# A planned queue order, in-place global keys and values, and matmuls of zeros at the start of an attention and feed-forward kernel

## The chip, the core and the metric

The kernel runs on one core of one Trainium2 chip. A core has engines that each execute their own instructions strictly in the order in which the program issues them, and that wait for one another by semaphores: TensorE (PE in the profile; PEld is its weight load), VectorE (DVE), ScalarE (ACT), GpSimd (POOL), and SyncE (SP), which here issues all DMA transfers. Transfers move data between the chip's memory and the on-chip SBUF; matmuls write to PSUM, which has eight banks of 2 KB per partition. The metric is the time of one execution on the device in microseconds (us); lower is better.

## The reference

Four batches, eight heads, 768 positions, head dimension 64. Each position attends to the last 96 positions (itself included) and to the first eight positions of its sequence, the global ones, with a bias that grows with the distance. The result is a matrix of 3072 tokens by 512, which goes through a feed-forward layer that takes the maximum of three products.

```python
rel = pos[:, None] - pos[None, :]
is_global = pos[None, :] < 8
is_local = (rel >= 0) & (rel < 96)
keep = is_global | is_local
dist = np.where(is_global & ~is_local, 96.0, np.abs(rel))
scores = q @ k.T / 8 - slopes[:, None, None] * dist      # per head
a = softmax(np.where(keep, scores, -1e9))
x = (a @ v).transpose(0, 2, 1, 3).reshape(3072, 512)
h = np.maximum(np.maximum(x @ w1, x @ w2), x @ w3)       # 512 -> 768
out = h @ w_out                                          # 768 -> 512
```

## The kernel before

The 3072 tokens are 24 tiles of 128, six per batch. A tile T attends to its own 128 keys and to the 128 keys before it (tile T-1, in which the first eight keys are replaced by the global ones, so that 128 columns hold both). A tile passes through these units, which the text names by a letter and the tile, with a half g of four heads after the point where there are two:

- **load** (L, line 108): three transfers of q, k and v, 256 KB each, into one of six buffers `raw`.
- **cast** (C, lines 110 to 117): POOL turns q and k into bf16 in one instruction (`qkb`) and v in a second (`va`).
- **X** (lines 139 to 151): eight PE transposes of q and k into PSUM, one ACT copy to `qkT`. Then POOL makes the key and value tiles that the *next* tile will see: `kgT`, a copy of the keys with the eight global columns laid over it (lines 136 and 137), and `vg`, the same for the values (lines 125 and 126).
- **S** (lines 153 to 183): eight small matmuls for four heads, an exponential on ACT into `P`. The multiplication of `P` by the mask `wmask` on DVE (line 182) is issued one unit later.
- **A** (lines 185 to 209): the product of `P` with the values of both tiles, then a reciprocal and a multiplication on DVE into `xb`.
- **T** (lines 211 to 220; the function is `u_XT`): four transposes and a DVE copy into `xT`.

The feed-forward layer works on chunks of tiles, of sizes 4, 2, 2, 4, 4, 4, 4. **F c.f.j** (line 231) is the product of chunk c with 128 columns of weight j: four matmuls that are 512 wide (256 in the chunks of two tiles). For j = 0 ACT copies the result, for j = 1 and 2 DVE takes the maximum with it (lines 238 and 240). **F2** (lines 243 to 252; O in the order of the change) is the second product of one tile: six 512-wide matmuls into the PSUM bank `po`, an ACT copy to `ost`, and a store.

The weights arrive in fp32 as three groups w0, w1 and w2 (three transfers of 512 KB each, one per j) and `w_out` (three of 512 KB). Their casts (W) are on ACT, DVE and POOL for j = 0, 1 and 2, those of `w_out` (Q) on ACT.

The order on the engines is the order in which the program issues its units, and so is the order of the loads in SP's queue. Line 318 lists the loads: tiles 0 to 3, w0, w1, tile 4, w2, tile 5, w_out, and then tiles 6 and on. X(T) is followed by the casts of tile T+1, and by the loads up to tile T+5 (lines 380 to 383). The attention units of all tiles form one list (lines 337 to 359), in which X of the next tile stands before the last units of the tile at hand: X4 stands before the second half of A3 and before T3. The attention units of chunk 0 go first; from then on they are spread evenly between the feed-forward units of the chunk before (lines 402 to 426). The second products of a chunk stand between the feed-forward groups of the next one; those of the last chunk come at the end, one after another.

The PSUM banks: `sp` two banks (scores), `h0`, `h1`, `h2` (feed-forward, and in the first four tiles also scores and transposes), `op`, `tp` (transposes of X and T), `po`.

Of the kernel before, what the change touches and what calls it, by code (L numbers as in the profile page):

```python
# [15 lines left out]
ALU = mybir.AluOpType  # L16


@with_exitstack
def kernel(  # L20
# [42 lines left out]
    kg_pool = ctx.enter_context(tc.tile_pool(name="kg", bufs=3))  # L63
# [23 lines left out]
    vg_ring = [persist.tile([128, H * 65], BF16, name=f"vg{i}") for i in range(3)]  # L87
# [4 lines left out]
    raw, qb, kb, qkT, kgT, Pt, ops, xb, rzs = {}, {}, {}, {}, {}, {}, {}, {}, {}  # L92
    xT = {}
    va, vg = {}, {}
# [14 lines left out]

    def cast(T):  # L110
        b, t = divmod(T, NT)
        r = raw[T]
        qk = cast_pool.tile([128, 2, DM], BF16, name="qkb", tag="qkb")
        qb[T] = qk
        nc.gpsimd.tensor_copy(qk, r[:, 0:2].rearrange("p a h d -> p a (h d)"))  # L115
        va[T] = va_first[b % 2] if t == 0 else va_ring[T % NVA]
        nc.gpsimd.tensor_copy(heads(va[T])[:, :, 0:D], r[:, 2])  # L117

    def make_vg(T):
        b, t = divmod(T, NT)  # L120
        if t == 0:
            vg[T] = va[T]
        elif t < NT - 1:
            vg[T] = vg_ring[T % 3]
            nc.gpsimd.tensor_copy(words(vg[T]), words(va[T]))
            nc.gpsimd.tensor_copy(words(vg[T][0:NG]), words(va[b * NT][0:NG]))

    def make_kg(T):
        b, t = divmod(T, NT)
        kT = qkT[T][:, 1]  # L130
        if t == 0:
            kgT[T] = kT
            nc.gpsimd.tensor_copy(kg8[b % 2], kT[:, :, 0:NG])
        elif t < NT - 1:
            kgT[T] = kg_pool.tile([128, NP, 128], BF16, name="kgT", tag="kgT")
            nc.gpsimd.tensor_copy(words(kgT[T]), words(kT))  # L136
            nc.gpsimd.tensor_copy(kgT[T][:, :, 0:NG], kg8[b % 2])

    def u_X(T):
        if T < NSTART and T % 2:  # L140
            tp = psH.tile([128, 2, NP, 128], BF16, name="tph", tag="h2")
        else:
            tp = psT.tile([128, 2, NP, 128], BF16, name="tp", tag="tp")
        for a in range(2):
            for jp in range(NP):
                nc.tensor.transpose(tp[:, a, jp], qb[T][:, a, jp * 128:(jp + 1) * 128], identb)  # L146
        qkT[T] = qkT_pool.tile([128, 2, NP, 128], BF16, name="qkT", tag="qkT")
        nc.scalar.copy(qkT[T], tp)  # L148
        make_kg(T)
        make_vg(T)  # L150
        return []

    def u_S(T, g):
        b, t = divmod(T, NT)
        alt = T < NSTART and g == 1
# [6 lines left out]
        for ds in range(2 if t else 1):  # L162
            for j2 in range(2):
                jp = 2 * g + j2
                for hh in range(2):
                    hsl = slice(64 * hh, 64 * hh + 64)
                    st = qkT[T][hsl, 1, jp] if ds == 0 else kgT[T - 1][hsl, jp]
# [13 lines left out]
        if t:  # L181
            return [lambda: nc.vector.tensor_mul(P, P, wmask[:, g])]  # L182
        return [lambda: nc.vector.tensor_mul(P[:, :, 0], P[:, :, 0], wmask0[:, g])]

    def u_A(T, g):
        b, t = divmod(T, NT)
        if T < NSTART and g == 1:
            op = psP.tile([128, 4, 65], FP32, name="opp", tag="po")
        else:
            op = psO.tile([128, 4, 65], FP32, name="op", tag="op")  # L190
        P = Pt[T, g]
        for j2 in range(2):
            for hh in range(2):
# [5 lines left out]
                if t:  # L199
                    nc.tensor.matmul(o, P[:, i, 1], heads(vg[T - 1])[:, h], start=False, stop=True,  # L200
                                     skip_group_check=True)
# [7 lines left out]
        return []  # L209

    def u_XT(T):
# [3 lines left out]
        tp = psT.tile([128, NP, 128], BF16, name="xtp", tag="tp")  # L215
# [4 lines left out]
        return []  # L220
# [4 lines left out]
    def u_F1(c, f, j):  # L225
# [15 lines left out]
        return []  # L241

    def u_F2(c, tt):
        po = psP.tile([128, DM], FP32, name="po", tag="po")
        for f in range(NF):
            nc.tensor.matmul(po, ht[c][:, f, tt * 128:(tt + 1) * 128], wo[:, f],  # L246
                             start=(f == 0), stop=(f == NF - 1))
        ost = ost_pool.tile([128, DM], FP32, name="ost", tag="ost")
        nc.scalar.copy(ost, po)  # L249
        T = chunks[c][tt]  # L250
        nc.sync.dma_start(out=out[T * 128:(T + 1) * 128, :], in_=ost)
        return []
# [5 lines left out]
    def load_w(g):  # L258
        for j in range(3):
            st = stage_pool.tile([128, 4, 256], FP32, name="wst", tag="wst")  # L260
            wst[g, j] = st
            nc.sync.dma_start(out=st, in_=wsrc[j][:, g * 256:(g + 1) * 256].rearrange(  # L262
                "(i p) f -> p i f", p=128))

    def load_wo():
        for i in range(3):
            st = stage_pool.tile([128, 2, DM], FP32, name="wst", tag="wst")
            wst["o", i] = st
            nc.sync.dma_start(out=st, in_=moe_w_out[i * 256:(i + 1) * 256, :].rearrange(
                "(i p) f -> p i f", p=128))  # L270

    def cast_w(g):
        nc.scalar.copy(w123[g][:, :, 0], wst[g, 0])
        nc.vector.tensor_copy(w123[g][:, :, 1], wst[g, 1])
        nc.gpsimd.tensor_copy(w123[g][:, :, 2], wst[g, 2])
# [3 lines left out]

    with tc.manual_schedule():  # L280
        load(0)

# [25 lines left out]
        for h in range(H):  # L308
# [8 lines left out]

        loads = [("T", T) for T in range(1, NSTART)] + [("w", 0), ("w", 1), ("T", NSTART),
                                                        ("w", 2), ("T", NSTART + 1), ("o",)]
        loads += [("T", T) for T in range(NSTART + 2, NTT)]  # L320
        done = [0]

        def upto(*what):
            if what[0] == "T" and what[1] >= NTT:
                return
            while what in loads[done[0]:]:
                x = loads[done[0]]
                done[0] += 1
                if x[0] == "T":
                    load(x[1])  # L330
                elif x[0] == "w":
                    load_w(x[1])
                else:
                    load_wo()


        att = []
        for i in range(NSTART):
            att.append(("X", i))
            if i >= 1:  # L340
                att += [("A", i - 1, 0), ("A", i - 1, 1)]
            att += [("S", i, 0), ("S", i, 1)]
            if i >= 1:
                att.append(("T", i - 1))
        i = NSTART - 1
        att += [("A", i, 0), ("X", i + 1), ("A", i, 1), ("S", i + 1, 0), ("T", i)]
        for i in range(NSTART, NTT + 1):
            if i < NTT and i > NSTART:
                att.append(("S", i, 0))
            if i > NSTART:  # L350
                att.append(("A", i - 1, 1))
            if i < NTT:
                att.append(("S", i, 1))
            if i + 1 < NTT:
                att.append(("X", i + 1))
            if i < NTT:
                att.append(("A", i, 0))
            if i > NSTART:
                att.append(("T", i - 1))

        deferred = []

        def tick():
            ready = [d for d in deferred if d[0] <= 0]
            rest = [(n - 1, fn) for n, fn in deferred if n > 0]
            deferred.clear()
            deferred.extend(rest)
            for _, fn in ready:
                fn()

        def emit_att(u):
            tick()
            if u[0] == "S":
                for fn in u_S(u[1], u[2]):
                    deferred.append((0, fn))
            elif u[0] == "A":
                u_A(u[1], u[2])
            elif u[0] == "X":
                T = u[1]
                u_X(T)  # L380
                if T + 1 < NTT:
                    cast(T + 1)
                upto("T", T + 5)
            else:
                u_XT(u[1])

        pos = 0

        def att_until(stop):
            nonlocal pos  # L390
            while pos < len(att):
                u = att[pos]
                emit_att(u)
                pos += 1
                if u == stop:
                    break

        upto("T", 3)
        cast(0)
        att_until(("T", chunks[0][-1]))  # L400
        cast_w(0)
        for c in range(NCH):
            ffn = []
            for f in range(NF):
                ffn += [(u_F1, (c, f, j)) for j in range(3)]
                if c and f >= 1 and f <= len(chunks[c - 1]):
                    ffn.append((u_F2, (c - 1, f - 1)))
            if c + 1 < NCH:
                end = att.index(("T", chunks[c + 1][-1])) + 1
            else:  # L410
                end = len(att)
                ffn += [(u_F2, (c, tt)) for tt in range(len(chunks[c]))]
            n = end - pos
            slots = len(ffn) - 2
            start = pos
# [47 lines left out]
```

## Time and profile before

| | us |
|---|---|
| median of three runs | 216.99 (216.52 to 217.34) |
| the profiled execution | 216.65 |
| its span, from first to last instruction | 214.9 |
| TensorE busy | 182.7 (85%) |
| VectorE busy | 121.5 (57%) |
| ScalarE busy | 113.0 (53%) |
| GpSimd busy | 66.1 (31%) |

The profile's times are those of one execution, counted from the first instruction. "Busy" counts the time in which an engine has an instruction at work; matmuls overlap, so that a full TensorE is not necessarily at its peak. In a row of the timeline the columns are the start, the duration, the engine, the source line, the operation, `out<-in`, the shapes and the count of merged instructions; in brackets stands how long the engine had idled before it, and what released it. In a row of groups the last columns are the busy time, the mean duration of one in ns, and the idle time in front of the group. In the chain of waits a row has only the start, the duration and what the time went to.

### The profile page before, as it was taken

What the parts mean: (1) busy time and instruction counts of PE and PEld (TensorE: products, weight loads), DVE (VectorE), ACT (ScalarE), POOL (GpSimd) and SP (SyncE); (2) the same over time, 40 slices, a digit from 0 to 9 for tenths busy, and PEclk for the clock granted to TensorE, in tenths of its full rate; (3) what the DMA queues carried; (4) which work ended last, traced back from release to release, by engine and by line L of the source; (5) the groups of instructions that cost most, each with busy time, mean ns of one, the idle gap of its engine ahead of it and who ended that gap; (6) DMA issues with size and microseconds to landing.
All of it is one profiled execution on the core that took longest, in us unless ns stands there. A gap on an engine that the chain in (4) does not pass through costs nothing.

```text
span 214.9 us, 4230 instructions
## 1 busy us (share of the span) xinstructions
PE 182.7 (85%) x1640; PEld 103.1 (48%) x1640; DVE 121.5 (57%) x266; ACT 113.0 (53%) x165; POOL 66.1 (31%) x131
## 2 busy tenths in 40 slices
PE   0446825998999999789999999999999999999962
PEld 0335622543566776466555455545544555444420
DVE  2164714576674648875876878565765666532400
ACT  5855504775765756566657635565564552233231
POOL 4654322437405047135433703135505000000000
PEclk9999999999999999999999999999999999999999
DMA  7999999999999894889547980111101111012122
GB/s 151 219 218 338 319 247 274 344 193 221 219 208 222 221 259 80 195 187 196 112 110 172 232 175 0 52 49 50 52 0 52 49 49 52 2 49 83 64 100 98
DMA packets 83924, 31.73 MB, mean 148 GB/s; under 512 B 75456, under 2 KB 80064, under 8 KB 83904
## 3 DMA queue, kind: packets, MB, share of 16 engines
q1 hardware_dynamic: 83904, 31.46, 64.1%
q8 instruction: 13, 0.21, 0.4%
q14 instruction: 7, 0.06, 0.1%
HBM read 25.17 MB, written 6.29 MB: 146 GB/s over the span
## 4 chain that ended last, share of the span: by engine, by line
PE 60%; SPq 17%; ACT 10%; DMA 4%; DVE 4%; issue 2%; POOL 1%; ACTq 0%
PE h L231 35%; PE po L246 14%; SPq L108 13%; ACT P L178 5%; DMA raw<-in_v_dram 4%; PE sp L168 4%; SPq L262 3%; DVE P L182 3%; PE xtp L218 2%; ACT qkT L148 2%; PE tp L146 2%; PE op L197 2%; ACT h L236 1%; ACT ost L249 1%; PE op L200 1%
## 5 line engine op out<-in xcount | busy, mean ns | idle before, releaser
L231 PE MATMUL h<-xT,w 128*128 128x512 bf16 (+1 forms) x504 | 110.7, 353 | 3.1 <-DVE xT L219 1.6
L231 PEld LDWEIGHTS <-w 128*128 128x128 bf16 x504 | 44.0, 98 | 35.9 <-issue 1.8
L178 ACT ACTIVATE P<-sp 128x1024 bf16<-128x1024 f32 (+1 forms) x44 | 42.1, 958 | 21.6 <-PE sp L168 21.6
L182 DVE TENSOR_TENSOR P<-P,wmask 128x1024 bf16<-128x1024 bf16 x40 | 33.6, 845 | 25.0 <-ACT P L178 24.6
L238 DVE TENSOR_TENSOR h<-h,h 128x512 bf16<-128x512 bf16 (+1 forms) x42 | 25.5, 608 | 29.0 <-PE h L231 28.4
L246 PE MATMUL po<-wo,ht 128*128 128x512 bf16 x144 | 35.0, 379 | 2.2 <-ACT ost L249 2.2
L236 ACT CAST h<-h 128x512 bf16<-128x512 f32 (+1 forms) x42 | 22.2, 528 | 22.5 <-PE h L231 22.2
L249 ACT COPY ost<-po 128x512 f32<-128x512 f32 x24 | 14.1, 586 | 37.2 <-PE po L246 34.1
L115 POOL CAST qkb<-raw 128x1024 bf16<-128x1024 f32 x24 | 24.8, 1034 | 15.7 <-DMA raw<-in_k_dram 15.7
L148 ACT COPY qkT<-tp 128x1024 bf16<-128x1024 bf16 x22 | 22.3, 1014 | 13.2 <-PE tp L146 13.2
L240 DVE TENSOR_TENSOR ht<-h,h 128x512 bf16<-128x512 bf16 (+1 forms) x42 | 25.5, 608 | 5.2 <-PE h L231 3.3
L146 PE MATMUL tp<-identb,qkb 128*128 128x128 bf16 x176 | 14.9, 234 | 13.6 <-POOL qkb L115 10.7
L136 POOL COPY kgT<-qkT 128x256 int32<-128x256 int32 x16 | 6.7, 416 | 59.7 <-ACT qkT L148 59.7
L146 PEld LDWEIGHTS <-qkb 128*128 128x128 bf16 x192 | 13.8, 108 | 19.8 <-POOL qkb L115 14.7
L246 PEld LDWEIGHTS <-ht 128*128 128x128 bf16 x144 | 13.2, 98 | 16.0 <-issue 3.0
L207 DVE TENSOR_TENSOR xb<-op,rz 128x256 bf16<-128x256 f32 x44 | 18.7, 424 | 1.5
L197 PEld LDWEIGHTS <-P 128*128 128x128 bf16 x192 | 15.0, 103 | 7.7 <-DVE xb L207 2.3
L168 PE MATMUL sp<-qkT 64*128 64x128 bf16 x204 | 14.1, 231 | 3.7 <-ACT qkT L148 2.9
L168 PEld LDWEIGHTS <-qkT 64*128 64x128 bf16 x224 | 7.6, 101 | 19.5 <-issue 15.7
L197 PE MATMUL op<-va,P 128*128 128x65 bf16 x148 | 14.6, 198 | 2.5 <-DVE xb L207 1.5
L200 PEld LDWEIGHTS <-P 128*128 128x128 bf16 x160 | 12.2, 103 | 2.4
L117 POOL CAST va<-raw 128x512 bf16<-128x512 f32 x20 | 12.7, 635 | 0.1
(52 smaller groups left out, 128.8 us busy)
## 6 DMA issues: line engine op xcount, KB each, us to landing
raw<-in_q_dram SPq DMA_DIRECT2D x24, 256.0 KB, 5.0
raw<-in_k_dram SPq DMA_DIRECT2D x24, 256.0 KB, 5.0
raw<-in_v_dram SPq DMA_DIRECT2D x24, 256.0 KB, 5.0
out_dram<-ost SPq DMA_DIRECT2D x24, 256.0 KB, 2.0
wst<-in_moe_w_dram SPq DMA_DIRECT2D x9, 512.0 KB, 6.5
wst<-in_moe_w_out_dram SPq DMA_DIRECT2D x3, 512.0 KB, 5.4
```

The source lines that it names most:

```text
L108: nc.sync.dma_start(out=r[:, i], in_=src[b, :, sl, :].rearrange("h s d -> s h d"))
L115: nc.gpsimd.tensor_copy(qk, r[:, 0:2].rearrange("p a h d -> p a (h d)"))
L146: nc.tensor.transpose(tp[:, a, jp], qb[T][:, a, jp * 128:(jp + 1) * 128], identb)
L148: nc.scalar.copy(qkT[T], tp)
L168: nc.tensor.matmul(sps[hh][:, j2, ds], st, qkT[T][hsl, 0, jp], start=True, stop=True, skip_group_check=True)
L178: nc.scalar.activation(P[:, :, 0:n], sp.rearrange("p a b d n -> p (a b) d n")[:, :, 0:n], AF.Exp, bias=0.0, scale=scale)
L182: return [lambda: nc.vector.tensor_mul(P, P, wmask[:, g])]
L197: nc.tensor.matmul(o, P[:, i, 0], heads(va[T])[:, h], start=True, stop=(t == 0), skip_group_check=True)
L231: nc.tensor.matmul(ps, w123[f // 2][:, dm, j, (f % 2) * 128:(f % 2) * 128 + 128], xT[c][:, dm], start=(dm == 0), stop=(dm == 3))
L238: nc.vector.tensor_max(h01s[c, f], h01s[c, f], ps)
L240: nc.vector.tensor_max(ht[c][:, f], h01s[c, f], ps)
L246: nc.tensor.matmul(po, ht[c][:, f, tt * 128:(tt + 1) * 128], wo[:, f], start=(f == 0), stop=(f == NF - 1))
```

## The change

The lists and counters that made the order are gone. A text, `SCHEDULE`, names 470 units, and a loop issues them in that order:

```python
units = {"L": load, "w": load_w, "o": load_wo, "C": cast, "X": u_X, "S": u_S, "M": u_M,
         "A": u_A, "G": put_kg, "V": put_vg, "T": u_XT, "F": u_F1, "W": cast_w,
         "Q": cast_wo, "O": u_F2, "E": u_E}
for u in SCHEDULE.split():
    units[u[0]](*(int(n) for n in u[1:].split(".") if n))
```

The units are finer than before: the casts of a tile are two (C T.0 for q and k, C T.1 for v), the mask multiplication is one of its own (M), so are the loads and casts of each weight (w, W) and the two copies of global keys (G) and values (V). Its beginning, and further parts of it:

```
C0.0 X0 L1 S0.0 C1.0 M0.0 S0.1 G0 X1 C0.1 S1.0 S1.1 M0.1 L2 C2.0 X2 M1.0 C1.1 G1 M1.1 A0.0 L3 C3.0
C2.1 A0.1 S2.0 S2.1 X3 L4 L5 M2.0 A1.0 A1.1 T0 w0.0 w0.1 G2 S3.0 M2.1 w0.2 w1.1 C4.0 V1 M3.0 X4 S3.1
A2.0 A2.1 M3.1 T1 G3 S4.0 w1.0 C3.1 w1.2 W0.0 L6 V2 w2.0 w2.1 C5.0 A3.0 A3.1 T2 M4.0 w2.2 L7 X5 S4.1
T3 F0.0.0 W0.1 F0.0.1 W0.2 F0.0.2 W1.1 F0.1.0 o0 C4.1 V3 F0.1.1 G4 F0.1.2 A4.0 W1.0 W1.2 S5.0 M4.1
M5.0 F0.2.0 C6.0 F0.2.1 A4.1 C5.1 F0.2.2 S5.1 M5.1 F0.3.0 V4 T4 F0.3.1 W2.0 F0.3.2 W2.1 o1 X6 F0.4.0
W2.2 A5.0 S6.0 F0.4.1 A5.1 S6.1 F0.4.2 F0.5.0 C7.0 T5 M6.0 F0.5.1 M6.1 X7 C6.1 C7.1 F0.5.2 A6.0 Q0
G6 F1.0.0 S7.0 F1.0.1 F1.0.2 F1.1.0 A6.1 F1.1.1 o2 Q2 M7.0 F1.1.2 F1.2.0 T6 S7.1 G7 L8 F1.2.1 A7.0
C8.0 Q1 L9 F1.2.2 F1.3.0 F1.3.1 M7.1 C9.0 X8 L10 O0.0 S8.0 L11 A7.1 C8.1 F1.3.2 M8.0 L12 L13 F1.4.0
F1.4.1 X9 S8.1 G8 M8.1 F1.4.2 O0.1 F1.5.0 S9.0 V7 F1.5.1 T7 A8.0 C10.0 L14 C9.1 M9.0 O0.2 X10 A8.1
...
F5.5.1 F5.5.2 T23 O4.3 F6.0.0 F6.0.1 F6.0.2 F6.1.0 F6.1.1 F6.1.2 F6.2.0 F6.2.1 O5.0 F6.2.2 O5.1
F6.3.0 F6.3.1 F6.3.2 O5.2 F6.4.0 O5.3 F6.4.1 F6.4.2 F6.5.0 F6.5.1 F6.5.2 E
```

The other parts, as diffs. The global keys and values are written into the tile's own buffers instead of copies, after its own attention has read them:

```diff
-            kgT[T] = kg_pool.tile([128, NP, 128], BF16, name="kgT", tag="kgT")
-            nc.gpsimd.tensor_copy(words(kgT[T]), words(kT))
-            nc.gpsimd.tensor_copy(kgT[T][:, :, 0:NG], kg8[b % 2])
+            nc.gpsimd.tensor_copy(kT[:, :, 0:NG], kg8[b % 2])
...
+    def put_vg(T):
+        b, t = divmod(T, NT)
+        if 0 < t < NT - 1:
+            nc.gpsimd.tensor_copy(words(va[T][0:NG]), words(va[b * NT][0:NG]))
```

For the first four tiles the cast of q moves to DVE, X always uses the bank `tp`, and T uses the bank `h2`:

```diff
-        nc.gpsimd.tensor_copy(qk, r[:, 0:2].rearrange("p a h d -> p a (h d)"))
...
+        if T < 4:
+            nc.vector.tensor_copy(qk[:, 0], flat[:, 0])
+            nc.gpsimd.tensor_copy(qk[:, 1], flat[:, 1])
+        else:
+            nc.gpsimd.tensor_copy(qk, flat[:, 0:2])
...
-        if T < NSTART and T % 2:
-            tp = psH.tile([128, 2, NP, 128], BF16, name="tph", tag="h2")
-        else:
-            tp = psT.tile([128, 2, NP, 128], BF16, name="tp", tag="tp")
+        tp = psT.tile([128, 2, NP, 128], BF16, name="tp", tag="tp")
...
+        where_xt = 'h2' if early(T) else 'tp'
```

The last chunk's second products go to four different banks, two tiles at a time, the sixth matmul of a tile after the first five of both; the copies of the last two tiles are split between ACT and DVE:

```diff
+    spare = ["po", "op", "tp", "sp"]
...
+            tag = spare[tt % 4] if c == last else "po"
...
+        if T >= NTT - 2:
+            for i, copy in enumerate((nc.scalar.copy, nc.vector.tensor_copy)):
+                sl = slice(i * 256, (i + 1) * 256)
+                copy(ost[:, sl], po[:, sl])
...
+    def u_E():
+        n = len(chunks[last])
+        for tt in range(0, n, 2):
+            two = range(tt, min(tt + 2, n))
+            for x in two:
+                f2_mm(last, x, range(NF - 1))
+            for x in two:
+                f2_mm(last, x, [NF - 1])
+                f2_out(last, x)
```

And right behind the first load, ahead of everything else, PE multiplies zeros:

```diff
         load(0)
+            zeros = persist.tile([128, 512], BF16, name="zeros")
+            nc.vector.memset(zeros, 0.0)
+            wp = psO.tile([128, 512], FP32, name="wp", tag="op")
+            for _ in range(13):
+                nc.tensor.matmul(wp, zeros[:, 0:128], zeros, start=True, stop=True)
```

The other strings of casts in POOL's order that the text below names stand in parts of `SCHEDULE` that are left out here.

More of the change, by code (lines that the diff above doesn't have):

```diff
@@ L19 @@
+"""
 @with_exitstack
@@ L240, in u_F1 @@
             nc.vector.tensor_max(ht[c][:, f], h01s[c, f], ps)
-        return []
-    def u_F2(c, tt):
[L244 to L252, printed above, removed]
+    pos_ = {}
@@ L254 @@
+    def u_F2(c, tt):
+        f2_mm(c, tt, range(NF))
+        f2_out(c, tt)
     wsrc = [moe_w1, moe_w2, moe_w3]
     wst = {}
[L258 to L270, printed above, removed]
@@ L315 @@
                                  scale=-slopes[h])
[L318 to L334, printed above, removed]
@@ L337 @@
[L337 to L359, printed above, removed]
@@ L361 @@
[L361 to L385, printed above, removed]
```

142 lines of the change are left out of this document (69 added, 73 removed).

## The prediction

> **What bounds the kernel now.** I read the slices of the page first (forty of 5.4 us), then the busy time by stage, then the chain of waits and the timeline where a stage is thin.
>
> ```profile
> PE   0446825998999999789999999999999999999962
> ```
>
> TensorE (PE) is nearly full from slice 9 on, and thin before. The same in five stages (columns: window, its length, then busy us of PE, PEld, DVE, ACT, POOL, the granted clock, DMA share, GB/s):
>
> ```profile
> 0.00:35.60 35.60, 15.16 (x176) 11.77 (x176) 14.85 (x40) 19.49 (x36) 15.83 (x39) 1.00 1.13 254
> 35.60:49.30 13.70, 12.23 (x97) 5.84 (x97) 8.09 (x17) 8.54 (x10) 5.34 (x7) 1.00 1.14 259
> 49.30:60.00 10.70, 10.70 (x78) 5.38 (x79) 6.91 (x15) 6.61 (x9) 6.12 (x10) 1.00 1.09 220
> 60.00:203.20 143.20, 138.88 (x1270) 77.99 (x1268) 90.98 (x194) 76.06 (x106) 38.78 (x76) 1.00 0.48 110
> 203.20:214.90 11.70, 5.70 (x25) 2.13 (x22) 0.69 (x1) 2.35 (x4) 0.00 (x0) 0.97 0.25 91
> ```
>
> The first 60 us have PE holes while the DMA share is full; from 60 to 203.2 us PE idles 143.20 - 138.88 = 4.3 us: no order of the same matmuls can take more than that out of this stage. The front and the tail are what can move. The front, from the timeline and, for the last three rows, the chain of waits:
>
> ```profile
> 29.68 1.04 POOL L115 CAST qkb<-raw 128x1024 bf16<-128x1024 f32 x1 [4.62 <-DMA raw<-in_k_dram]
> ...
> 30.78 1.03 PE L146 MATMUL tp<-identb,qkb 128*128 128x128 bf16 x8 [4.00 <-POOL qkb L115]
> ...
> 35.28 0.42 DVE L219 COPY xT<-xtp 128x512 bf16<-128x512 bf16 x1
> ...
> 35.75 1.86 PE L231 MATMUL h<-xT,w 128*128 128x512 bf16 x4 [1.64 <-DVE xT L219]
> ...
> 40.42 1.03 PE L231 MATMUL h<-xT,w 128*128 128x512 bf16 x4
> ...
> 60.05 0.69 DVE L240 TENSOR_TENSOR ht<-h,h 128x512 bf16<-128x512 bf16 x1
> ```
>
> ```profile
> 38.79 8.79 DMA raw<-in_v_dram
> ...
> 47.64 0.62 POOL vaf L117
> ...
> 48.26 0.99 POOL w L275
> ```
>
> Tile 4's loads stand in SP's queue behind two weight groups, so its cast starts at 29.68. Its transposes stand in PE's order ahead of tile 3's last attention and ahead of T3, whose copy is the row at 35.28, and the first feed-forward group (F0.0.0) starts only at 35.75. Then the weight cast at 48.26, which F0.2.2 needs, stands in POOL's order behind a cast of tile 6 that waits for its load: PE stops until 49.30. Chunk 0's feed-forward ends with the maximum at 60.05.
>
> ```profile
> 6.51 1.03 PE L146 MATMUL tp<-identb,qkb 128*128 128x128 bf16 x8 [6.51 <-POOL qkb L115]
> ...
> 7.75 0.99 ACT L148 COPY qkT<-tp 128x1024 bf16<-128x1024 bf16 x1
> ```
>
> Those two rows are tile 0's start: its transposes and their copy.
>
> **The front after the change.** Bytes decide it: a tile is 3 x 256 KB = 0.786 MB, a weight group (three transfers) 1.57 MB. The DMA rates by window, same columns:
>
> ```profile
> 2.00:16.00 14.00, 4.69 (x52) 3.65 (x53) 5.03 (x13) 9.23 (x25) 7.30 (x15) 1.00 1.32 222
> 16.00:26.00 10.00, 7.23 (x88) 5.66 (x87) 6.28 (x14) 5.67 (x8) 4.25 (x10) 1.00 1.11 336
> 26.00:30.00 4.00, 0.62 (x8) 0.46 (x8) 1.64 (x5) 0.35 (x1) 0.32 (x1) 1.00 1.04 175
> ```
>
> Tiles 0 to 3 (3.1 MB) land by 16 us at 222 GB/s; the weights that follow move at 336; tile 4's remainder crawls at 175, and from 49.3 on tiles run at 220 (stage row). The new SP order is tiles 0 to 5, w0, w1, tile 6, w2, tile 7, w_out, tile 8. Six tiles: 2 + 4.72/0.222 = 23.3 us. w0 lands at 23.3 + 1.57/0.336 = 28.0, w1 at 32.7, tile 6 at 36.2 (222 GB/s) to 37.2 (175), w2 at 40.9 to 41.9, tile 7 at 45.4. The unit lengths (groups of instructions, then the chain of waits):
>
> ```profile
> L178 ACT ACTIVATE P<-sp 128x1024 bf16<-128x1024 f32 x37 | 38.0, 1026 | 17.3 <-PE sp L168 17.2
> L148 ACT COPY qkT<-tp 128x1024 bf16<-128x1024 bf16 x22 | 22.3, 1014 | 13.2 <-PE tp L146 13.2
> L273 ACT CAST w<-wst 128x1024 bf16<-128x1024 f32 x3 | 3.1, 1044 | 0.0
> L275 POOL CAST w<-wst 128x1024 bf16<-128x1024 f32 x3 | 3.1, 1039 | 0.0
> L274 DVE CAST w<-wst 128x1024 bf16<-128x1024 f32 x3 | 2.1, 685 | 0.0
> ```
>
> ```profile
> 50.55 0.86 PE h L231 x4
> ...
> 68.91 0.33 PE sp L168 x8
> ...
> 73.06 0.45 PE tp L146 x8
> ...
> 88.75 0.44 PE h L231 x4
> ...
> 199.35 1.29 PE po L246 x6
> ```
>
> Attention of tiles 0 to 3 is off the end's path as long as it keeps step with the loads. ACT is its fullest engine: a tile takes a copy of 1.01 and two exponentials of 1.03, 3.1 us, against 0.786/0.222 = 3.5 us for its load. It takes up tile 0 at 7.75, after the mask's exponentials, and would be through S4.0 at about 23 (the short tile 0 some 2.5, tiles 1 to 3 with their waits 3.5 each, then the copy of X4 and one exponential), 1 us and more ahead of w0.0 (23.3 + 1.6 = 24.9). F0.0.0 then waits for ACT's weight cast, 24.9 + 1.04 = 25.9; F0.0.2 for POOL's, 28.0 + 1.04 = 29.1, and ends at 30.0. From there 15 groups of 0.86 (12.9 us) and, in PE's order, A4, A5, S5, S6, T4, T5, X6, X7 remain before F0.5.2 ends: two X at 0.45, two S at 0.33, two shorter S and four A and two T at about 0.25 each (estimates, scaled from the 0.33 and 0.45), 3.5 us. Together 16.4 us, 46.4. (Check: the old kernel did 10 groups and 8 such units in its full stage 49.30 to 60.00, 8.6 + 1.9 = 10.5 of 10.7 us.) The last cast of w2 bounds it from the other side: 41.9 + 1.04 = 42.9, and F0.4.2 to F0.5.2 with T5 and X7 is 4.1 us behind, 47.0. I take 47.0, and 47.5 with the clock below: **12.4 us** earlier than 59.95, with the same work done but one short A. Bounds: 45.5 (weights at the 360 or so that 336 averages down) to 53 (loads at 175 after every weight group, and the cold groups).
>
> **The zeros.** Thirteen 512-wide matmuls at 1.86/4 = 0.46 us cold take 6.0 us, beginning about 1 us in, when PE has nothing to do (first transposes at 6.5). Worst cost: 0.6 us of delay to X0, hidden, since ACT's copy of X0 cannot start before 7.75. What they bring: the groups at 35.75 (1.86) and 40.42 (1.03) are the same instruction, slow before and quick after some 4 us of dense PE work, while the granted-clock column says 1.00 in both windows. If PE is slow at 25.9, F0.0.0 to F0.0.2 run back to back at 1.86 and end near 31 instead of 30.0: 1 us. If it is quick, nothing. I take 0.5. The Trainium skill, "TensorE: Matmul & The Clock Gate", Part 1, says the array runs at half rate until about 3.4 us of sustained work and falls back after an idle window of that length. By that rule the zeros' warmth is gone by the first 3.4 us gap among the loads, and the sum would be 0.5 us worse than mine; the trace agrees with the rule's first half (4 us), and shows gaps of 4.00 us at 30.78 with slow matmuls behind.
>
> **In-place keys and values.** Gone are the copies to kgT and vg, per tile 0.40 + 0.41 us on POOL, 16 of each:
>
> ```profile
> L136 POOL COPY kgT<-qkT 128x256 int32<-128x256 int32 x16 | 6.7, 416 | 59.7 <-ACT qkT L148 59.7
> L125 POOL COPY vg<-va 128x260 int32<-128x260 int32 x16 | 6.5, 406 | 0.0
> ```
>
> 13.2 us of POOL, off the path (POOL is busy 38.78 of 143.20): worth 0 by itself. The small copies stay and now wait: G(T), which overwrites eight keys, for S(T.1), and S(T+1) waits for G(T); V(T) for A(T.1), and A(T+1) for V(T). Behind them in POOL's queue stand casts of later tiles. From tile 6 on the PE work standing between S(T.1) and S(T+1.0) in the written order is at least 1.5 us, between A(T.1) and A(T+1.0) at least 1.2, against at most 0.41 for the copy: 0, unless a 1.03 or 0.61 cast stands just ahead, then up to 0.5 a tile.
>
> **The middle.** Loads first: tile 7 lands at 45.4, w_out at 50.1, the keys of tile 8 at 52.5, and the cast ends at 53.6. PE comes to X8 11 groups of 0.44 and 1.4 us of attention after F0.5.2, at 53.8: level. X9 is about 3.6 us behind both ways. So 0 to 3 us of waiting, I take 1; from tile 11 on the loads run ahead, also where an output transfer stands before a load in SP's queue (O0.0 before L11). The written order leaves S, A, X and T of a tile apart by more than their ACT and DVE steps almost everywhere, so of the 4.3 us idle I take 3 back. Against it, DVE:
>
> ```profile
> 84.19 2.87 DVE L182 TENSOR_TENSOR P<-P,wmask 128x1024 bf16<-128x1024 bf16 x1
> ...
> 87.53 0.68 DVE L182 TENSOR_TENSOR P<-P,wmask 128x1024 bf16<-128x1024 bf16 x1
> ```
>
> ```profile
> 84.93 1.03 POOL L115 CAST qkb<-raw 128x1024 bf16<-128x1024 f32 x1
> 85.91 0.61 POOL L117 CAST vaf<-raw 128x512 bf16<-128x512 f32 x1
> ```
>
> The mask multiply takes 2.87 instead of 0.68 while POOL runs casts one after another, and ends 0.5 us after the last of them (85.91 + 0.61): 2.2 us lost. The new POOL order has such rows (C13.0 C14.0 C12.1 C13.1; C15.1 C16.1 C17.1 C17.0; C19.0 C18.1 C20.0 C21.0), 3 to 4 us each. PE can work on for some 1 to 2 us; I take 1 us in all. The middle: 3 - 1 - 1 = **1 us**, bounds -4 and +4.3.
>
> **The tail.**
>
> ```profile
> 203.07 1.46 PE L246 MATMUL po<-wo,ht 128*128 128x512 bf16 x6
> ...
> 204.61 0.59 ACT L249 COPY ost<-po 128x512 f32<-128x512 f32 x1 [2.48 <-PE po L246]
> 205.25 1.46 PE L246 MATMUL po<-wo,ht 128*128 128x512 bf16 x6 [0.72 <-ACT ost L249]
> ...
> 211.13 0.59 ACT L249 COPY ost<-po 128x512 f32<-128x512 f32 x1 [1.59 <-PE po L246]
> ```
>
> Four output groups share one PSUM bank, so each waits for the copy before it: 203.24 to 211.72, 8.5 us. With four banks: 4 x 1.29 = 5.2, plus 0.2 for the last matmul to drain (1.46 - 1.29), plus a copy halved over ACT and DVE, 0.3 to 0.6, with semaphores 5.9. The wait for the last maximum (0.69) is covered by ten matmuls of two groups. The last two stores now come together: 0.2 back. **2.4 us**, bounds 1.8 to 2.8.
>
> **Sum.** The profiled execution took 216.65 us, 1.75 beside its span of 214.9; the median of the runs is 0.34 above it. 12.4 + 1 + 2.4 = 15.8: 200.9 on that scale, 201.2 on the median's; I forecast **201.0 us**, own range 198 to 205.
>
> **Rivals.** (a) Late loads: tiles at 175 GB/s after weights, not 222, cost 1 us each for tiles 6 to 8, and the waits at X8 to X10 grow by 3: 205 to 209. For it 26 to 30 us; against it 220 GB/s from 49.3 on. Chance 0.12. (b) The mask multiply behind strings of casts: 2.2 us lost on DVE, less 1 us of cover, 1.2 on PE each. Three to five such cases give 4 to 6 us, 204.6 to 207; chance 0.13. The Trainium skill, "SBUF — State Buffer", says in its sections on contention that a VectorE instruction with two SBUF inputs and a GpSimd instruction that reads SBUF exclude one another; the rows at 84 us agree (2.87 against 0.68). (c) The same mechanism on the other side: slower than before needs over 15 us, 13 of the 30 multiplies from tile 7 on, each held by a cast. With 13.2 us of copies gone, POOL has fewer to hold them with. Chance 0.04, about 218 to 222. Within 0.5% of before (a bit more than a measurement here can tell from none): 0.03. (d) The middle gives back all 4.3 us and the front reaches 45.5: 14.4 + 4.3 + 2.6 = 21.3, 195.7; say 195 to 198; chance 0.13. My forecast keeps 0.55. Range: 196 to 208, which leaves out the slow tenth and part of (d). Faster: 0.55 + 0.12 + 0.13 + 0.13 = 0.93.
>
> **What would show it.** F0.0.0 near 26, F0.0.2 waiting for its POOL cast near 29, the last 512-wide maximum of chunk 0 at 47 to 48 instead of 60.05; PE busy over 97% from there to the last feed-forward group at about 189; mask multiplies of over 2 us beside POOL casts in few places; 5.9 us from there to the end of the last copy. The forecast is wrong if tile 5 lands after 25 us, if PE waits over 3 us in total at X8 to X10, or if A waits for P behind casts in more than five places.

## The result and the profile after

The changed kernel takes 203.0 us (median of four, 200.93 to 205.54) against 217.0 us: a ratio of 0.9325, 95% interval 0.9246 to 0.9403. Six later executions gave 203.36 us (202.13 to 205.7). The forecast was 201.0 us with a range of 196 to 208. The ratio, here and below, leaves out executions that lie over 1.5% above the fastest of the same kernel, and one of them is the profiled execution: 205.54 us, the longest of its four, with a span of 203.8. Where its stages differ from those of a second profile of the same kernel (span 201.4), that is said.

The busy time by stage, with the same borders as before: start of the first feed-forward group, last maximum of chunk 0, last maximum of the last chunk.

```profile
0.00:30.55 30.55, 19.93 (x205) 13.46 (x206) 15.12 (x46) 20.89 (x38) 11.66 (x28) 0.68 1.12 225
30.55:52.53 21.98, 21.89 (x157) 10.80 (x157) 15.19 (x30) 10.72 (x15) 9.23 (x13) 0.89 1.09 282
52.53:194.10 141.57, 139.67 (x1272) 79.64 (x1269) 93.53 (x196) 79.88 (x110) 32.87 (x58) 0.99 0.57 124
194.10:203.80 9.70, 5.14 (x24) 2.16 (x22) 1.44 (x3) 1.72 (x4) 0.00 (x0) 0.93 0.28 108
```

The reader is to see three gains. Chunk 0 ends at 52.53 instead of 60.05: 7.5 us. The middle takes 141.57 us, where the old trace had 203.27 - 60.05 = 143.2: 1.65 us. The tail takes 9.7 instead of 11.6 us: 1.9. Together 11.1, which is the difference of the spans. In the second profile the front gives 8.3, the middle 3.3, the tail 1.9.

The front, in the timeline of the changed kernel:

```profile
1.19 4.58 PE L349 MATMUL wp<-zeros 128*128 128x512 bf16 x13 [1.19 <-DVE zeros L346]
...
5.60 0.69 PE L181 MATMUL tp<-identb,qkb 128*128 128x128 bf16 x8
...
21.37 1.04 POOL L158 CAST qkb<-raw 128x1024 bf16<-128x1024 f32 x1 [3.41 <-DMA raw<-in_k_dram]
...
27.93 1.06 PE L181 MATMUL tp<-identb,qkb 128*128 128x128 bf16 x8
...
30.11 0.42 DVE L256 COPY xT<-xtp 128x512 bf16<-128x512 bf16 x1 [0.72 <-PE xtp L255]
...
30.59 7.59 PE L267 MATMUL h<-xT,w 128*128 128x512 bf16 x24 [0.52 <-DVE xT L256]
30.73 1.30 POOL L326 CAST w<-wst 128x1024 bf16<-128x1024 f32 x1 [4.24 <-DMA wst<-in_moe_w_dram]
...
52.53 0.69 DVE L276 TENSOR_TENSOR ht<-h,h 128x512 bf16<-128x512 bf16 x1 [0.22 <-PE h L267]
```

Tile 4's keys are there at 21.37, 8.3 us earlier than before, but the units behind them follow one another in a chain that ends with X5 (27.93) and T3 with its copy (30.11), and the first feed-forward group starts at 30.59, not at the forecast 25.9. Its first 24 matmuls take 7.59 us; at 0.86 for four they would take 5.2.

The zeros warm TensorE early, and it does not last. The granted clock, by windows:

```profile
8.00:10.00 2.00, 1.12 (x16) 0.68 (x16) 0.32 (x2) 1.62 (x4) 1.14 (x3) 1.00 1.36 218
10.00:12.00 2.00, 0.78 (x16) 0.75 (x16) 1.22 (x3) 1.32 (x3) 0.19 (x1) 0.82 1.35 217
12.00:30.00 18.00, 12.84 (x158) 9.92 (x153) 10.98 (x27) 11.80 (x16) 7.54 (x12) 0.50 1.14 247
...
34.00:36.00 2.00, 2.00 (x8) 0.79 (x7) 1.06 (x2) 0.00 (x0) 0.66 (x1) 0.71 1.17 203
```

From about 11 to 35 us the clock is at half. (The old profile says 1.00 over its whole front, where the same group took 1.86 us at 35.75 and 1.03 at 40.42. So a share of 1.00 ahead of the first change that a profile records says nothing.)

In the middle one place stands out. POOL and DVE in the timeline, and TensorE after them:

```profile
116.74 0.40 POOL L172 COPY va<-vaf 8x260 int32<-8x260 int32 x1 [5.91 <-PE op L236]
...
117.09 1.03 POOL L158 CAST qkb<-raw 128x1024 bf16<-128x1024 f32 x1
117.11 4.09 DVE L217 TENSOR_TENSOR P<-P,wmask 128x1024 bf16<-128x1024 bf16 x1
...
118.08 0.61 POOL L149 CAST vaf<-raw 128x512 bf16<-128x512 f32 x1
...
118.64 2.02 POOL L158 CAST qkb<-raw 128x1024 bf16<-128x1024 f32 x2
...
121.81 0.28 PE L255 MATMUL xtp<-identb,xb 128*128 128x128 bf16 x2 [1.26 <-DVE xb L243]
...
123.93 1.01 PE L181 MATMUL tp<-identb,qkb 128*128 128x128 bf16 x8 [0.51 <-DVE xT L256]
124.74 1.91 PE L267 MATMUL h<-xT,w 128*128 128x512 bf16 x4
```

POOL idles 5.91 us until A16 frees the values that V16 overwrites, and then runs V16 and four casts in one string to 120.66. The mask multiply of tile 17 starts 0.02 us after the first cast and ends 0.5 us after the last: 4.09 instead of 0.68 us. TensorE stops for 1.26 and 0.51 us, and then, in this execution, a group takes 1.91 us: the clock is at half for 3.4 us more.

### The profile page after: what moved, and what is told of

The parts are those of the page before. It is cut to its first block, busy times and chain, and to the rows that moved or that the text cites. A ratio compares the mean times of both kernels' runs of the same rounds, so it can differ in the third digit from the quotient of the medians.

```text
span 203.8 us, 4266 instructions
## 1 busy us (share of the span) xinstructions
PE 186.6 (92%) x1653; PEld 106.1 (52%) x1653; DVE 125.3 (61%) x273; ACT 113.2 (56%) x165; POOL 53.8 (26%) x99
## 3 DMA queue, kind: packets, MB, share of 16 engines
HBM read 25.17 MB, written 6.29 MB: 154 GB/s over the span
## 4 chain that ended last, share of the span: by engine, by line
PE 76%; DVE 8%; SPq 6%; DMA 3%; issue 2%; ACT 1%; POOL 1%; DVEq 0%; POOLq 0%; ACTq 0%
PE h L267 44%; PE po L288 15%; SPq L142 6%; PE sp L200 6%; PE tp L181 5%; DVE P L217 4%; DMA raw<-in_k_dram 3%; PE xtp L255 3%; PE op L233 3%; PE op L236 2%; DVE h L274 1%; DVE ht L276 1%; DVE xb L243 1%; DVE xT L256 1%; POOL qkb L158 1%
## 5 line engine op out<-in xcount | busy, mean ns | idle before, releaser
L267 PE MATMUL h<-xT,w 128*128 128x512 bf16 (+1 forms) x504 | 107.6, 356 | 0.6 <-DVE xT L256 0.5
L267 PEld LDWEIGHTS <-w 128*128 128x128 bf16 x504 | 46.5, 99 | 39.1 <-issue 4.4
L183 ACT COPY qkT<-tp 128x1024 bf16<-128x1024 bf16 x24 | 24.3, 1012 | 13.1 <-PE tp L181 12.1
L158 POOL CAST qkb<-raw 128x1024 bf16<-128x1024 f32 x20 | 20.7, 1042 | 13.9 <-DMA raw<-in_k_dram 9.3
L200 PE MATMUL sp<-qkT 64*128 64x128 bf16 x324 | 17.8, 230 | 4.5 <-ACT qkT L183 4.4
L181 PE MATMUL tp<-identb,qkb 128*128 128x128 bf16 x192 | 17.4, 238 | 4.5 <-POOL qkb L158 3.2
L243 DVE TENSOR_TENSOR xb<-op,rz 128x256 bf16<-128x256 f32 x44 | 18.7, 425 | 1.5
L200 PEld LDWEIGHTS <-qkT 64*128 64x128 bf16 x352 | 11.0, 101 | 15.1 <-issue 7.1
L181 PEld LDWEIGHTS <-qkb 128*128 128x128 bf16 x192 | 13.5, 106 | 9.4 <-POOL qkb L158 3.4
L233 PEld LDWEIGHTS <-P 128*128 128x128 bf16 x192 | 14.9, 103 | 4.8 <-DVE P L217 1.3
L167 POOL COPY qkT<-kg 128x32 bf16<-128x32 bf16 x16 | 3.8, 236 | 44.0 <-PE sp L200 42.7
L242 DVE RECIPROCAL rz<-op 128x4 f32<-128x4 f32 x44 | 7.8, 178 | 11.4 <-PE op L236 9.5
L149 POOL CAST va<-raw 128x512 bf16<-128x512 f32 x20 | 13.5, 680 | 4.3 <-PE op L236 4.3
```

Source lines behind the costliest of these rows:

```text
L158: nc.gpsimd.tensor_copy(qk, flat[:, 0:2])
L200: nc.tensor.matmul(sps[hh][:, j2, ds], st, qkT[T][hsl, 0, jp], start=True, stop=True, skip_group_check=True)
L233: nc.tensor.matmul(o, P[:, i, 0], heads(va[T])[:, h], start=True, stop=(t == 0), skip_group_check=True)
L267: nc.tensor.matmul(ps, w123[f // 2][:, dm, j, (f % 2) * 128:(f % 2) * 128 + 128], xT[c][:, dm], start=(dm == 0), stop=(dm == 3))
```

## The experiments

The 95% intervals are of the ratio to the kernel before, which ran beside each group of four; runs of different groups are best compared by their ratios.

| run | median us (range, count) | ratio, interval |
|---|---|---|
| after_again | 203.36 (202.13 to 205.7, 6) | 0.9342, 0.9312 to 0.9372 |
| no_zeros | 202.52 (201.15 to 204.48, 6) | 0.9295, 0.9266 to 0.9325 |
| zeros_gap | 202.82 (201.31 to 203.41, 6) | 0.9320, 0.9288 to 0.9352 |
| pool_spread | 204.54 (203.25 to 205.7, 6) | 0.9417, 0.9381 to 0.9452 |
| string_ahead | 203.15 (201.65 to 205.25, 6) | 0.9317, 0.9287 to 0.9348 |
| copies_back | 200.58 (199.94 to 200.66, 4) | 0.9222, 0.9204 to 0.9241 |
| tail_old | 203.59 (203.32 to 205.66, 6) | 0.9394, 0.9358 to 0.9430 |
| before_loads | 213.92 (213.83 to 214.46, 4) | 0.9848, 0.9829 to 0.9866 |
| cb_no_zeros | 200.14 (199.19 to 201.4, 6) | 0.9224, 0.9192 to 0.9256 |
| cb_tail_old | 202.97 (202.38 to 203.22, 4) | 0.9346, 0.9327 to 0.9366 |
| cb_tail_whole | 200.35 (199.3 to 201.72, 6) | 0.9236, 0.9206 to 0.9266 |
| v_back | 201.19 (198.69 to 205.01, 6) | 0.9236, 0.9196 to 0.9276 |

And the stages of their traces, from the start rows of the same maxima (us; one profiled execution each): the first feed-forward group, the granted clock from 28 to 30 us (a dash where no change is recorded before), the last maximum of chunk 0, the stretch from chunk 3's to chunk 4's last maximum, in which the 4.09 us multiply lies, and the tail.

| run | first group | clock at 28 to 30 | chunk 0 ends | chunk 3 to 4 | tail |
|---|---|---|---|---|---|
| before | 35.75 | - | 60.05 | other order | 11.6 |
| changed, first profile | 30.59 | 0.50 | 52.53 | 35.1 | 9.7 |
| after_again | 30.21 | 0.50 | 51.74 | 33.6 | 9.7 |
| no_zeros | 29.49 | - | 51.51 | 35.1 | 9.7 |
| zeros_gap | 28.68 | 1.00 | 50.04 | 33.6 | 9.6 |
| pool_spread | 28.59 | 1.00 | 49.53 | 35.0 | 9.7 |
| string_ahead | 29.28 | 1.00 | 49.36 | 31.6 | 9.6 |
| copies_back | 29.48 | 1.00 | 49.93 | 31.1 | 9.7 |
| tail_old | 30.33 | 0.50 | 52.36 | 33.6 | 11.6 |
| before_loads | 34.91 | 0.68 | 57.38 | other order | 11.6 |
| v_back | 30.64 | 0.50 | 52.66 | 31.1 | 9.7 |
| cb_no_zeros | 28.21 | - | 49.73 | 31.1 | 9.7 |
| cb_tail_old | 29.41 | 1.00 | 50.19 | 31.1 | 11.6 |
| cb_tail_whole | 29.17 | 1.00 | 49.90 | 31.1 | 9.4 |

The front of the planned order comes in two forms: where the clock is up by 28 us, chunk 0 ends at 49.4 to 50.2, and where it stays at half until 34 or 35 us, at 51.7 to 52.7. pool_spread, string_ahead and tail_old have the changed kernel's front unaltered and fall on both sides; why an execution takes one form or the other was not tried.

**after_again: the changed kernel once more.**

> The changed kernel once more, as the measure for the runs beside it. Theory: its times spread over some 4 us (200.9 to 205.5 so far) because TensorE's clock warms at different moments, so the mean granted clock of an execution and its time go together, about 0.3 us for each 0.0024 of clock. Rival: the spread has another source (the chip, the loads), and clock and time don't go together.

The clock shares of the six were 0.940, 0.941, 0.971, 0.940, 0.938 and 0.972, their times 203.13, 203.94, 202.45, 203.58, 205.70 and 202.13. The two with the most clock are the two shortest, by 0.7 to 1.8 us against the three at 0.940 and 0.941; by the theory's 0.3 us for each 0.0024 of clock it would be 4 us. And at 0.940 and 0.941 the times still lie 0.8 us apart. The clock is part of the spread and not all of it.

**no_zeros: without the 13 matmuls.**

```diff
...
-            for _ in range(13):
-                nc.tensor.matmul(wp, zeros[:, 0:128], zeros, start=True, stop=True)
```

> The 13 matmuls of zeros are left out, all else as changed. Theory: their warmth is gone by about 11 us, long before the first feed-forward group at 30 us, so the median stays within 1 us of the changed kernel's, and the first transposes take 1.03 instead of 0.69 us at no cost. Rival: they bring the later warm-up forward, and without them the kernel is 1 to 3 us slower.

202.52 against 203.36 us, with intervals that overlap: the zeros bring nothing that can be measured.

**zeros_gap: eight zeros more, where TensorE waits for tile 4.**

```diff
-    ... C4.0 V1 M3.0 X4 S3.1
+    ... C4.0 V1 M3.0 z X4 S3.1
+            wq = psP.tile([128, 512], FP32, name="wq", tag="po")
+            for _ in range(8):
+                nc.tensor.matmul(wq, zeros[:, 0:128], zeros, start=True, stop=True)
```

> Eight more matmuls of zeros stand ahead of X4, where TensorE waits for tile 4's load. Theory: the first feed-forward groups ran at half clock (24 matmuls in 7.6 us instead of 5.2); kept busy there, the clock is up before 30 us, the first six groups take 5.3 us, and the median falls by 2 to 3 us. Rival: the front is bound by loads and casts, the matmuls wait for weights anyway, and the time stays within 0.5 us; a worse rival: the zeros run late and push X4, plus 0.5 to 1 us.

Chunk 0 ends 1.7 us earlier than in after_again, as the theory wants, but the median falls by 0.5 us only, with intervals that overlap. That the added zeros brought the earlier end is not shown: pool_spread and string_ahead, without them, end chunk 0 at 49.53 and 49.36, and the clock is up at 28 us in their profiles too. The chain of waits of this run shows where the gain goes:

```profile
47.19 8.83 DMA raw<-in_k_dram
...
56.48 1.05 POOL qkb L158
...
57.58 0.62 PE tp L181 x8
```

Tile 8's keys land at 56.0; its cast follows, and X8 starts at 57.58. TensorE is busy 8.97 of the ten microseconds there:

```profile
50.00:60.00 10.00, 8.97 (x111) 6.55 (x108) 6.53 (x17) 7.65 (x12) 1.85 (x3) 1.00 0.95 218
```

Chunk 1's last maximum comes at 70.06, against 70.40 in after_again: 0.3 us is left of 1.7. In pool_spread and string_ahead, where the cast of tile 8 starts at 55.23 and 54.74 instead of 56.48, it comes at 68.80 and 68.31, and more is left. What a faster clock in the front is worth hangs on when tile 8's keys land.

**pool_spread: the string broken behind G18.**

```diff
...
-  C19.0 S18.0 C18.1 C20.0 T16 A17.0 F4.1.2 L23 X19 F4.2.0 S18.1 O3.0 C21.0 C22.0 C19.1 M18.0 M18.1 A17.1 C20.1 G18 S19.0 F4.2.1 X20 O3.1 X21 M19.0
+  C19.0 S18.0 C18.1 T16 A17.0 F4.1.2 L23 X19 F4.2.0 S18.1 O3.0 C19.1 M18.0 M18.1 A17.1 G18 C20.0 S19.0 F4.2.1 X20 C21.0 O3.1 X21 C20.1 C22.0 M19.0
...
```

> In POOL's order C20.0, C21.0, C20.1 and C22.0 move behind G18, so that the string C19.0 C18.1 C20.0 C21.0 is broken; all else as changed. Theory: the mask multiply of tile 17 no longer takes 4.09 us, TensorE's stall of 1.8 us near 121 us and the half clock after it (124 to 127 us) are gone: 2.5 to 4 us faster. Rival: another multiply meets another string, or the stall was this one execution's, and the median moves by less than 1 us.

1.2 us slower in the medians, 1.6 by the ratios. The edit missed: G18 is the first tile of a batch, where G only reads the keys and waits for no S, so nothing held the casts back and one more got into the string. The multiply became longer:

```profile
115.23 4.80 DVE L215 TENSOR_TENSOR P<-P,wmask 128x1024 bf16<-128x1024 bf16 x1
...
120.64 0.38 PE L253 MATMUL xtp<-identb,xb 128*128 128x128 bf16 x2 [1.97 <-DVE xb L241]
```

4.80 for 4.09 us on DVE, 1.97 for 1.26 us of stall on TensorE: an unmeant dose that fits.

**string_ahead: three casts moved ahead of V16.**

```diff
-    F4.0.1 M17.0 A16.1 C18.0 X18 F4.0.2 V16 S17.1 M17.1 F4.1.0 F4.1.1 C19.0 S18.0 C18.1 C20.0 T16 A17.0
+    F4.0.1 M17.0 A16.1 C18.0 C19.0 C18.1 C20.0 X18 F4.0.2 V16 S17.1 M17.1 F4.1.0 F4.1.1 S18.0 T16 A17.0
```

> C19.0, C18.1 and C20.0 stand ahead of V16 in POOL's order, so that they run while POOL idles and only C21.0 is left behind V16; all else as changed. Theory: the mask multiply of tile 17 takes under 2 us instead of 4.09, the stall of 1.8 us near 121 us goes, and with it the 3.4 us of half clock that follows in some executions: 1.5 to 3.5 us faster than the changed kernel's 203.4. Rival: TensorE's wait there has another last cause (tile 18's copy, the exponentials), and less than 0.7 us goes.

The stretch from chunk 3 to 4 falls by 1.9 us, but the median stays. The casts now pile up one tile earlier, behind V15 and G16, and hold another multiply, so that the stretch from chunk 2's to chunk 3's last maximum is 27.4 us, where after_again has 23.8:

```profile
106.57 0.39 POOL L172 COPY va<-vaf 8x260 int32<-8x260 int32 x1 [2.21 <-PE op L236]
106.92 0.20 POOL L167 COPY qkT<-kg 128x32 bf16<-128x32 bf16 x1
107.07 2.01 POOL L158 CAST qkb<-raw 128x1024 bf16<-128x1024 f32 x2
```

```profile
107.45 3.72 DVE L217 TENSOR_TENSOR P<-P,wmask 128x1024 bf16<-128x1024 bf16 x1
```

That turned the suspicion from the order of the casts to the waits of V and G ahead of them.

**copies_back: the in-place writes undone, the order kept.**

```diff
-            nc.gpsimd.tensor_copy(kT[:, :, 0:NG], kg8[b % 2])
+            kgT[T] = kg_pool.tile([128, NP, 128], BF16, name="kgT", tag="kgT")
+            nc.gpsimd.tensor_copy(words(kgT[T]), words(kT))
+            nc.gpsimd.tensor_copy(kgT[T][:, :, 0:NG], kg8[b % 2])
...
+            vg[T] = vg_ring[T % 3]
+            nc.gpsimd.tensor_copy(words(vg[T]), words(va[T]))
...
```

> The in-place writes are undone: POOL copies keys and values to kgT and vg again (0.40 + 0.41 us a tile), in the planned order. Theory: POOL is off the path, so within 0.7 us of the changed kernel. Rival: the planned order lives on a lean POOL; the copies lengthen the strings that hold the mask multiply, and it is 2 to 5 us slower.

Both were wrong: it is 2.8 us faster in the medians (200.58 against 203.36) and 2.6 by the ratios, whose intervals lie apart, and all four executions lie within 0.7 us. POOL is busy 72.6 us instead of 54.8 in after_again, and TensorE does not stop anywhere from chunk 3 to 4 (31.1 instead of 33.6 us). The whole difference of the two profiles lies there: chunk 3's last maximum comes at 111.66 here and 111.89 in after_again, chunk 4's at 142.76 and 145.45. Its multiplies, all 40 (duration in ns, least, median, most):

```profile
L223 DVE TENSOR_TENSOR P<-P,wmask x40: 681/684/1533, 12.9 to 163.1; 128x1024 bf16<-128x1024 bf16 x40
```

against the second profile of the changed kernel:

```profile
L217 DVE TENSOR_TENSOR P<-P,wmask x40: 681/684/4089, 12.9 to 165.8; 128x1024 bf16<-128x1024 bf16 x40
```

**v_back: only the values copied again.**

> Only the values are copied again (vg); the keys stay in place. Theory: the stall came from casts piling up behind V, which waits for A in POOL's queue; without that wait no multiply takes over 2.5 us, and the median is that of copies_back, 200.0 to 200.9. Rival: the keys' writes G, which wait for S, pile up casts as well, and it stays at 202 to 203.5.

```diff
+            vg[T] = vg_ring[T % 3]
+            nc.gpsimd.tensor_copy(words(vg[T]), words(va[T]))
-            nc.gpsimd.tensor_copy(words(va[T][0:NG]), words(va[b * NT][0:NG]))
+            nc.gpsimd.tensor_copy(words(vg[T][0:NG]), words(va[b * NT][0:NG]))
...
```

```profile
L220 DVE TENSOR_TENSOR P<-P,wmask x40: 681/685/1401, 12.7 to 164.2; 128x1024 bf16<-128x1024 bf16 x40
```

No multiply takes over 1.4 us, and the stretch from chunk 3 to 4 is 31.1 us, as in all five kernels that copy the values: the stall is V's wait. The median, 201.19, lies 0.3 above the expected band, and by the ratios v_back and copies_back can't be told apart. The profiled execution has the slower form of the front (chunk 0 ends at 52.66). The keys' wait G alone cost nothing visible here.

**cb_no_zeros, cb_tail_old, cb_tail_whole: the small terms, on the steadier kernel.**

> copies_back (in-place writes undone, planned order) without the 13 matmuls of zeros, on this kernel since its times spread by only 0.7 us. Theory: the zeros are worth nothing, within 0.5 us of copies_back's 200.6. Rival: they bring the later warm-up forward, and it is 1 us slower or more.

> copies_back with the old tail (one PSUM bank, whole ACT copies). Theory: 1.9 us slower than copies_back, 202.5, as the stretch from the last maximum to the end shows (11.6 against 9.7 us). Rival: less than 1 us slower, as the medians with the changed kernel suggested (203.6 against 203.4).

> copies_back, but the last two tiles' output copies aren't split: tile 22's is whole on ACT, tile 23's whole on DVE. Theory: in the split form DVE's half waited for ACT's half (199.11 to 199.49, then 199.51), so the two engines took turns; whole copies run side by side and the last ends 0.3 to 0.4 us earlier, 200.2. Rival: two engines can't copy out of PSUM side by side there, and it is the same or 0.3 us slower.

The zeros: 200.14 without, 200.58 with them, one interval within the other; nothing. The tail: 202.97 with the old one, 2.4 us more, of which the tail's own stretch shows 1.9 (11.6 against 9.7). Its profile shows a loss elsewhere, too:

```profile
94.73 3.36 DVE L223 TENSOR_TENSOR P<-P,wmask 128x1024 bf16<-128x1024 bf16 x1 [0.39 <-ACT P L216]
```

Here a multiply met a string of four casts on POOL (94.79 to 97.50) although the values are copied, and the stretch from chunk 2 to 3 is 25.15 us, against 23.71 in copies_back. In copies_back the same string ran from 97.31 to 100.01, and no multiply waited for all of it. So the copies take away the string that V's wait makes, and not every such meeting. Whole copies instead of halves:

```diff
-            for i, copy in enumerate((nc.scalar.copy, nc.vector.tensor_copy)):
-                sl = slice(i * 256, (i + 1) * 256)
-                copy(ost[:, sl], po[:, sl])
+            (nc.scalar.copy if T == NTT - 2 else nc.vector.tensor_copy)(ost, po)
```

In copies_back the halves, and in cb_tail_whole the whole copies, at the end of the timeline:

```profile
194.02 0.65 ACT L304 COPY ost<-po 128x256 f32<-128x256 f32 x2 [1.52 <-issue]
194.43 0.76 DVE L304 COPY ost<-po 128x256 f32<-128x256 f32 x2 [4.73 <-ACT ost L304]
```

```profile
193.11 0.59 ACT L302 COPY ost<-po 128x512 f32<-128x512 f32 x1 [1.52 <-issue]
193.28 0.69 DVE L302 COPY ost<-po 128x512 f32<-128x512 f32 x1 [4.49 <-PE po L294]
```

DVE's first half waits for ACT's, which writes the same tile `ost` (the row names ACT's write to `ost` as the releaser; whether the program or the chip makes this wait is open); whole, the two run side by side and the stretch from the last maximum to the end is 9.4 instead of 9.7 us. In the medians (200.35 and 200.58) that can't be told from nothing.

**tail_old and before_loads: one part of the change by itself.**

> The last four tiles' second products go through one PSUM bank again, with one ACT copy each; all else as changed. Theory: 2.0 us slower (the stretch from the last maximum to the end is 9.7 us in the changed kernel, 11.6 in the old one). Rival: the split copies and the two late stores give most of it back, under 1 us slower.

On the changed kernel the old tail's stretch is 11.6 us, 1.9 more, but the median only 0.2 more, lost in the spread of both; by the ratios it is 1.1 us. cb_tail_old is the better measurement.

> The kernel before with one edit: SP loads tiles 4 and 5 ahead of w0 and w1, tile 6 ahead of w2 and tile 7 ahead of w_out, as the changed kernel does. Theory: most of the front's gain is this order, since X4 and T3 no longer wait behind weights: the first feed-forward group starts near 30 instead of 35.75, chunk 0 ends 5 to 8 us earlier, and the median is 211 to 213. Rival: the old unit order makes POOL's weight casts wait behind tile casts, and under 3 us remain.

```diff
-        loads = [("T", T) for T in range(1, NSTART)] + [("w", 0), ("w", 1), ("T", NSTART),
-                                                        ("w", 2), ("T", NSTART + 1), ("o",)]
-        loads += [("T", T) for T in range(NSTART + 2, NTT)]
+        loads = [("T", T) for T in range(1, 6)] + [("w", 0), ("w", 1), ("T", 6),
+                                                   ("w", 2), ("T", 7), ("o",)]
+        loads += [("T", T) for T in range(8, NTT)]
```

3.5 us faster than before, between the two theories; the first group starts at 34.91, hardly earlier, and chunk 0 ends 2.7 us earlier, against 8.3 us in after_again. The load order alone is the smaller part; the front needs the rest of the change with it. Which part of the rest (the unit order, the cast of q on DVE, the banks of X and T) was not run.

The best version measured is the planned order with the copies of keys and values kept, about 200.4 us with or without the zeros and with either split of the last copies: 1.4% under the changed kernel.

## Why the prediction was right, and where it was not

The direction, the three places and the range held; the time was 2.0 us over the forecast. In spans the gain was 11.1 and 13.5 us, not 15.8: the front fell short by 4 to 5 us, and the middle gave more than forecast. By its terms:

**Front: 12.4 forecast, 7.5 and 8.3 in the two profiles.** The step that failed is "Six tiles: 2 + 4.72/0.222 = 23.3 us. w0 lands at ... 28.0", a landing worked out from bytes over a mean rate. The windows of the changed kernel:

```profile
2.00:16.00 14.00, 9.18 (x87) 5.46 (x86) 5.85 (x17) 10.57 (x27) 5.03 (x11) 0.83 1.31 220
16.00:20.00 4.00, 2.87 (x36) 2.14 (x34) 2.85 (x8) 3.16 (x5) 1.78 (x3) 0.50 1.35 220
20.00:24.00 4.00, 1.54 (x17) 1.15 (x18) 0.74 (x2) 0.77 (x2) 1.42 (x3) 0.50 0.95 192
24.00:30.00 6.00, 5.45 (x70) 4.43 (x69) 4.63 (x12) 4.57 (x7) 2.10 (x4) 0.50 1.00 322
```

The bytes up to tile 4's keys, 3.67 MB, had moved by 18.7 us, but the cast that waited for them started at 21.37. The bytes up to the last part of w0, 6.29 MB, had moved by 28.9, and its cast started at 30.73. The two casts started 2.7 and 1.8 us after the mean stream had passed their bytes; what makes the lag was not tried. The cast of w0's first part, forecast at 24.9, started at 27.52, on its load. The second half of the miss is "through S4.0 at about 23, 1 us and more ahead": tile 4's late landing made the chain X4, S3.1, A3, X5, S4.1, T3 the last to end, at 30.11, and not w0. The third is the clock, taken at 0.5 us: 24 matmuls lost 2.4. In size: dense matmuls began 3.1 us later than forecast (30.59 against 27.4, which is 30.0 less three groups) and lost 1.9 us more to the clock. What of this last part survives tile 8's load differs: 0.3 us of 1.7 in zeros_gap, 1.6 of 2.2 in pool_spread.

**The zeros.** The forecast gave them half a microsecond, and nothing was found. The Trainium skill, "TensorE: Matmul & The Clock Gate", Part 1, says that an idle window of about 3.4 us brings half rate back. The trace agrees that the clock falls back, full at 8 to 10 us and half from about 11 on, and differs in the length. The gaps behind the zeros stand in brackets:

```profile
8.78 0.29 PE L200 MATMUL sp<-qkT 64*128 64x128 bf16 x4 [2.49 <-ACT qkT L183]
...
11.22 0.59 PE L200 MATMUL sp<-qkT 64*128 64x128 bf16 x8 [1.29 <-ACT qkT L183]
```

Neither reaches that length: sparse work was enough.

**In-place: 0 forecast, a loss of 2.6 to 2.8 us found.** The step that failed is "0, unless a 1.03 or 0.61 cast stands just ahead, then up to 0.5 a tile". It asked what delays the copy and who waits for the copy. What it passed over is what the copy delays: with V waiting for A, all casts behind it collect, and then run as one string. The forecast had the price of such a string (the multiply held for 2.2 us) named this one among three and had its length right (3 to 4 us; 3.6 found), but took the strings from the written order and 1 us for all of them. copies_back has the same written order, and there this multiply takes 0.68 us: V's wait makes the string, and it cost 2.5 us.

**Middle: 1 us forecast, 1.65 and 3.3 found.** Within its bounds, but partly by luck: a larger recovery and a larger loss cancel. copies_back, without V's stall, has its last maximum at 189.01 and needs 139.1 us from chunk 0's end, 4.1 less than before; and this although it waits longer for tile 8 (19.9 us from chunk 0's to chunk 1's last maximum, 18.7 in the changed kernel's first profile). The stall takes 2.5 us back, and 1.5 more where half clock follows it.

**Tail: 2.4 forecast; 1.9 in the stretch, 2.4 in the medians of copies_back and cb_tail_old.** The mis-sized step is the halved copy, "0.3 to 0.6": the halves took turns, and whole copies give 0.3 us back. The rest is the end of the stores, which comes 3.5 us after the last copy instead of 3.2, where the forecast took 0.2.

**Rivals.** Of (a), late loads, the mechanism was there from the first tiles on and is in the front's miss. Of (b) one multiply over 2 us came in the middle, not three to five. (c) and (d) did not come. In the first profile TensorE did not stop at X8 to X10, and in zeros_gap it waited 1.03 us for X8; TensorE was busy 139.67 of 141.57 us in the middle, 98.7%.

## What to carry to other kernels

An in-order queue that gets a new wait holds everything behind it, and what has been held then comes in one string: ask what a string of that engine does to its neighbours, even if the engine is idle most of the time. Saving a fourth of the work of an engine that is off the path (54.8 instead of 72.6 us) was worth less than nothing, since the copy it saved was also a buffer that kept GpSimd from waiting for TensorE. When a load's arrival decides a stage, take the arrival from rows of waiting casts and not from bytes over a mean rate.

## What the runs showed of the hardware

A DVE multiply with both operands in SBUF, started 0.02 us after a POOL cast, got no turn between four casts that followed one another: 4.09 us for 0.68. The Trainium skill, "SBUF — State Buffer", section "Who interferes with whom", describes the shared ports as a lock that the second to issue waits for until the first finishes; here the wait went on through three more POOL instructions that were issued later than the multiply. And a stall of 1.26 and 0.51 us on TensorE at 121 us was followed in some executions (the first profile, with 0.50 at 124 to 126 us, and no_zeros) by 3.4 us of half clock, and in others (after_again and zeros_gap, with 1.00 there) by none, with the same stall: 1.5 us of the stretch from chunk 3 to 4 (35.1 against 33.6) hang on that.
